# Quartered up products, a ring of chunks and moved side work in a fused retention and mixer kernel

## The chip, the cores and the metric

The kernel runs on one core of a Trainium2 chip. A core has a matrix engine (TensorE, PE in the profile, with its weight loads as PEld), three elementwise engines (VectorE: DVE, ScalarE: ACT, GpSimd: POOL) and SyncE (SP), which here issues DMAs. Each engine runs its own list of instructions in order; semaphores make one wait for another. Matrix products go into PSUM, which has eight banks, each one 128x512 tile of 32-bit floats; the other engines read them from there into SBUF. The metric is the device time of one execution, in microseconds (us), as the median of several runs; lower is better.

## The reference, cut to what matters

```python
def _attn_ref(q, k, v):                      # 8 batches, 8 heads, 576 tokens, 64 dims
    scores = scale * np.matmul(q, k.transpose(0, 1, 3, 2))
    gamma = 1.0 - 2.0 ** (-5.0 - np.arange(H))
    Dmat = np.where(rel >= 0, gamma[:, None, None] ** rel[None, :, :], 0.0)
    return np.matmul(scores * Dmat[None, :, :, :], v)

def _moe_ref(x, U, V, w_ch1, w_ch2):         # x: 8 batches, 576 tokens, 512
    xt = x.transpose(0, 2, 1)
    h = xt @ U @ V                           # rank 32, over the tokens
    u = x + h.transpose(0, 2, 1)
    ch = np.maximum(u @ w_ch1, 0.0) @ w_ch2  # 512 -> 2048 -> 512
    return u + ch
```

So: attention with a decay in place of the softmax gives x; a low-rank mixer over the tokens gives u; two dense layers with a relu between them, the larger part of the work, give the output.

## The kernel before, in words

A batch has 576 tokens, four and a half chunks of 128. Two batches make a *pair* of nine chunks. The dense layers run over *tiles* of four chunks (512 tokens), nine tiles in all, so a tile can lie in one pair or across two.

**The order of the work.** Nothing is reordered on TensorE, VectorE or ScalarE: the program writes the order out by hand. Batches 0 and 1 and tile 0 are written as a list of short steps, `EARLY` (lines 33 to 64), done by `early` (line 605). In it `dn` is the mixer's down product (tokens to rank 32) of a head pair, `at` copies it out of PSUM, `ux` and `uv` build the transposed u of a head pair in PSUM (x through the identity, plus V times the down product), `ua` and `ub` copy it to SBUF. `hu` is the up product of one chunk of batch 0 in the plain layout, `ha` adds x to it, which gives u. `y`, `R`, `M` and `O` are work of tile 0: a first product, a relu, a unit of four matmuls, an output add with its store. `misc` is a list of setup work, mostly on VectorE (`between`, line 1311), `hv` issues the loads of batch 1's k and v on SP's queue.

After that, the loop at line 1343 runs over tiles 1 to 8. Tile j is a list of *units* (`mlp_units`): 16 units of the first layer (four 128x512 products each), then units of the second layer, 16 of four matmuls in tile 1, and 14 in the later tiles, where sums of blocks of the weights and of the first layer's result save products (seven products instead of eight). `sums_of_w2` (line 894) makes those of the weights, six VectorE instructions, once, within tile 1. Into the units the attention of batch j + 1 is threaded: `attention_steps` (line 568) gives each step a number, and a step runs before the unit of that number. A *visit* is the work on a head pair: products of the last pair's values, new states and scores, which VectorE masks. The last visit is followed by the mixer: `mix_middle` (down product), `mix_up_full` (the up product of four chunks) and `mix_up` (the chunk that is half a batch), VectorE's adds of x, and `mix_turn_by_dma`, DMA transposes of u into uT on SP's queue. uT is the first layer's moving operand of the next tile, u is added to its output. What is left of batch 1 (plain u of chunks 4 to 8) is in a list `late`, done within tile 1.

**Rank 32 on a 128-row engine.** From batch 2 on, `mix_up_full` uses `at_diag`: the down product of head pair g lies in rows 32g to 32g+31 and columns 128g to 128g+127, and V is repeated in all four row groups, so each product needs 32 rows only, and four row groups can hold four of them. For batches 0 and 1 the down product lies in `at_sb`, over 128 rows padded with zeros, and an up product takes the whole engine.

**Where u lives.** `pair_pool` holds u and uT of a pair, in two sets that alternate. In a tile across two pairs, `first` (line 943) makes two groups of four products for each unit, one for each pair's chunks (128 and 384, 256 and 256, or 384 and 128 columns), and some later additions of u are split in the same way.

**PSUM banks.** In the loop three banks (`ps_mm`, tag "mm") serve the units, three ("one", tag "att") and two ("two", tag "pss") the attention. A bank is given out in turn; the next user waits until the last reader is done.

Of the kernel before, what the change touches and what calls it, by code (L numbers as in the profile page):

```python
# [14 lines left out]
class Pinned:  # L15
# [52 lines left out]
def kernel(  # L68
# [19 lines left out]
    dm = H * D  # L88
# [44 lines left out]
    pair_pool = ctx.enter_context(tc.tile_pool(name="pair_pool", bufs=2))  # L133
# [168 lines left out]

    def scale_head(b, h):

        x = v_sets[b % NSET][:, :, h, :]
        act.activation(out=x, in_=x, func=AF.Copy, scale=vs64[:, h:h + 1])

    to_scale = []
# [27 lines left out]
    def wait_for_turns(b):  # L336

        chs = chunks_of(b)
        pool.tensor_copy(
            out=landed[:, 0:len(chs)], in_=pairs[b // 2]["uT"][:, chs[0]:chs[-1] + 1, 0, 0]  # L340
        )
# [169 lines left out]
    def mix_up(b, m, x_t, st, pair):  # L511
# [3 lines left out]
        ch = m if b % 2 == 0 else NB - 1 + m  # L515
        dve.tensor_tensor(
            out=pair["u"][lo:hi, ch, :], in0=ps[lo:hi, :], in1=x_t[lo:hi, m, :], op=ALU.add
        )

    def mix_up_full(b, x_t, st, pair):  # L520
# [3 lines left out]
        ps += [banks["one"].tile([P, dm], FP32, tag="att", name="ps_h") for _ in range(2)]  # L524
        first = b % 2
# [8 lines left out]
        ch = 0 if b % 2 == 0 else NB  # L534
        for g in range(NHP):
            cols = slice(g * P, (g + 1) * P)
            dve.tensor_tensor(
                out=pair["u"][:, ch:ch + NB - 1, cols],
                in0=ps[g].rearrange("p (c d) -> p c d", c=NB - 1),
                in1=x_t[:, first:first + NB - 1, cols], op=ALU.add,  # L540
            )

    def mix_turn(ch, pair):
        ps = banks["one"].tile([P, NCC, P], BF16, tag="att", name="ps_ut")
        for cc in range(NCC):
            pe.transpose(ps[:, cc, :], pair["u"][:, ch, cc * P:(cc + 1) * P], ident)
        act.copy(out=pair["uT"][:, ch, :, :], in_=ps)

    def mix_turn_by_dma(chs, pair):

        a, b = chs[0], chs[-1] + 1
        sp.dma_start_transpose(
            out=pair["uT"][:, a:b, :, :].rearrange("p c k t -> p (c k) t"),
            in_=pair["u"][:, a:b, :].rearrange("p c d -> p (c d)"),
        )

    pairs = {}
# [847 lines left out]
```

## Time and profile before

| | us |
|---|---|
| median of 3 runs | 316.35 |
| lowest and highest | 316.05, 318.78 |
| the profiled execution | 315.44 |
| its span, first to last instruction | 313.7 |
| VectorE busy | 227.8 |
| mean DMA rate (GB/s) | 129 |

The profiled execution is one more run; between its time and its span lie 1.74 us of start and end. In a row of the timeline the first number is the start in us from the first instruction, the second the length, then engine, operation, output, inputs and shape; x is the count of merged instructions, and in brackets stands how long the engine had been idle and what released it. "L25" is the line of a helper that records every operation, so groups are told apart by the names of their tiles: `ps_y` and `y_t` are the dense layers, `w_sb` the weights, `kv_runs` from tile 1 on the sums of w2, `ps_b` the PSUM banks of the early list, `xh`, `pss`, `sc` and `ret` the visits, `ps_at` and `ps_h` the mixer, `u_t` and `uT_t` u and its transpose. Matmuls are pipelined: each is shown with a tail that overlaps the next one, and the distance of two starts tells the rate.

### The profile page before, as it was taken

The numbers are of one execution on the slowest core, as the hardware profiler recorded it, in microseconds if no ns is written. First come the engines' busy times: TensorE is split into PE (matmuls) and PEld (weight loads), VectorE is DVE, ScalarE is ACT, GpSimd is POOL, SyncE is SP. The second block draws the span as 40 slices with busy tenths as digits, with TensorE's granted clock in tenths as the row PEclk, the third lists the DMA queues.
The fourth block names the chain that finished last, engine by engine and source line by source line (L and its number), as shares of the span: only waits on it lengthen the run. The fifth ranks groups of instructions, "written<-read, shape, count | busy, mean of one in ns | idle before, by whom it ended". The sixth has DMA issues, their size and how long they took to land.

```text
span 313.7 us, 9760 instructions
## 1 busy us (share of the span) xinstructions
PE 305.0 (97%) x4120; PEld 203.5 (65%) x4120; DVE 227.8 (73%) x551; ACT 163.5 (52%) x338; POOL 136.5 (44%) x177
## 2 busy tenths in 40 slices
PE   8899999999998999999999999999999999999995
PEld 3664456644543677845788888457877884685484
DVE  6877529859997896899689968997799772352244
ACT  7667514367521687267726772678077407504610
POOL 8682339948940971289139812612200220040040
PEclk9999999999999999999999999999999999999999
DMA  8999999999999999599999999994510051012003
GB/s 121 198 206 207 201 204 138 160 178 169 135 149 229 116 148 153 119 170 127 151 203 148 155 135 166 145 149 94 167 36 4 2 154 66 0 34 102 0 2 135
DMA packets 154525, 40.59 MB, mean 129 GB/s; under 512 B 139089, under 2 KB 153457, under 8 KB 154481
## 3 DMA queue, kind: packets, MB, share of 16 engines
q0 software_dynamic: 91344, 17.09, 69.8%
q1 hardware_dynamic: 63136, 22.88, 37.9%
q8 instruction: 32, 0.52, 0.7%
q14 instruction: 13, 0.10, 0.1%
HBM read 36.85 MB, written 9.44 MB: 148 GB/s over the span
## 4 chain that ended last, share of the span: by engine, by line
PE 80%; DVE 7%; DMA 3%; SPq 3%; issue 1%; ACT 0%; DVEq 0%; ACTq 0%
PE ps_y L25 66%; PE xh L25 5%; PE ps_b L25 4%; SPq L25 3%; DVE u_t L25 2%; DMA kv_runs<-in_v_dram 2%; PE sc L25 2%; DMA uT_t<-u_t 2%; PE pss L25 1%; DVE kv_runs L25 1%; PE ps_h L25 1%; DVE v_all L25 1%; DVE o_sb L25 1%; PE ps_at L25 1%; DVE V_sb L25 1%
## 5 line engine op out<-in xcount | busy, mean ns | idle before, releaser
L25 PE MATMUL ps_y<-uT_t,w_sb 128*128 128x512 bf16 (+3 forms) x768 | 130.8, 326 | 1.4 <-DMA uT_t<-u_t 1.4
L25 ACT ACTIVATE y_t<-ps_y 128x512 bf16<-128x512 f32 x144 | 85.6, 597 | 63.5 <-PE ps_y L25 62.4
L25 PEld LDWEIGHTS <-w_sb 128*128 128x128 bf16 x768 | 68.3, 98 | 52.3 <-DMA uT_t<-u_t 1.6
L25 POOL TENSOR_TENSOR o_sb<-o_sb,u_t 128x512 f32<-128x512 f32 (+1 forms) x24 | 24.4, 1034 | 109.4 <-DVE o_sb L25 102.2
L25 PEld LDWEIGHTS <-y_t 128*128 128x128 bf16 x576 | 55.3, 98 | 18.7
L25 PE MATMUL ps_y<-w_sb,y_t 128*128 128x256 bf16 (+1 forms) x352 | 57.7, 311 | 0.0
L25 DVE SCALAR_TENSOR_TENSOR S<-S,keep,pss 128x64 bf16<-128x64 bf16 x168 | 47.0, 280 | 5.1
L25 DVE TENSOR_TENSOR o_sb<-ps_y,o_sb 128x512 f32<-128x512 f32 (+1 forms) x37 | 24.4, 662 | 26.8 <-PE ps_y L25 12.8
L25 DVE TENSOR_TENSOR ret<-sc,qsrow 128x640 bf16<-128x640 f32 x48 | 39.3, 820 | 3.9 <-ACT y_t L25 2.1
L25 PEld LDWEIGHTS <-y_sums 128*128 128x128 bf16 x336 | 32.0, 98 | 4.7
L25 POOL DMA_DIRECT2D k_all<-in_k_dram x36 | 30.8, 859 | 8.9 <-DMA w_sb<-in_moe_w_ch_dram 7.6
L25 POOL DMA_DIRECT2D q_all<-in_q_dram x37 | 28.9, 806 | 4.2 <-DMA w_sb<-in_moe_w_ch_dram 4.2
L25 DVE TENSOR_TENSOR y_sums<-y_t 128x512 bf16<-128x512 bf16 x28 | 11.7, 420 | 22.2 <-ACT y_t L25 22.1
L25 POOL DMA_DIRECT2D v_all<-in_v_dram x31 | 27.3, 888 | 0.5 <-PE ps_y L25 0.2
L25 PE MATMUL ps_y<-w_sb,y_sums 128*128 128x256 bf16 x224 | 27.4, 273 | 0.0
L25 PE MATMUL ps_y<-kv_runs,y_t 128*128 128x256 bf16 x224 | 26.9, 273 | 0.0
L25 ACT ACTIVATE x_t<-xh,xs 128x320 bf16<-128x320 f32 x48 | 22.7, 524 | 7.9 <-PE xh L25 6.2
L25 DVE TENSOR_TENSOR u_t<-ps_h,x_t 128x512 bf16<-128x512 f32 (+1 forms) x35 | 22.3, 682 | 3.0 <-PE ps_h L25 2.8
L25 ACT CAST S<-pss 128x64 bf16<-128x64 f32 x24 | 5.0, 208 | 27.3 <-issue 24.1
L25 ACT ACTIVATE v_all<-v_all,vs 128x320 bf16<-128x320 bf16 x32 | 14.9, 548 | 0.1
L25 POOL COPY landed<-uT_t 128x4 bf16<-128x4 bf16 (+1 forms) x4 | 0.8, 191 | 32.2 <-DMA uT_t<-u_t 32.2
L25 PE MATMUL ps_y<-kv_runs,y_sums 128*128 128x256 bf16 x112 | 13.9, 273 | 0.0
(132 smaller groups left out, 307.7 us busy)
## 6 DMA issues: line engine op xcount, KB each, us to landing
out_dram<-o_sb SPq DMA_DIRECT2D x35, 256.0 KB, 3.0
w_sb<-in_moe_w_ch_dram POOLq DMA_DIRECT2D x8, 512.0 KB, 12.2
v_all<-in_v_dram POOLq DMA_DIRECT2D x25, 128.0 KB, 6.9
k_all<-in_k_dram POOLq DMA_DIRECT2D x24, 128.0 KB, 6.0
q_all<-in_q_dram POOLq DMA_DIRECT2D x20, 128.0 KB, 4.8
q_all<-in_q_dram POOLq DMA_DIRECT2D x12, 144.0 KB, 5.8
given<-in_v_dram SPq DMA_DIRECT2D x8, 128.0 KB, 4.4
kv_runs<-in_v_dram SPq DMA_DIRECT2D x3, 256.0 KB, 6.1
```

The source lines that it names most:

```text
L25: return self._tc.keep_in_program_order(call(*args, **kwargs))
```

## The change

Five edits, in the words of the program:

1. **Up products in row quarters for batches 0 and 1.** In `EARLY`, `hu` and `ha` of chunks 0 to 3 go. A new step `hd` (behind `misc`) copies the four diagonal blocks of `at_sb` into `at_diag[0]` on VectorE; `hf`, between M 10 and M 11, makes the 16 products of `mix_up_full`, into four of the early banks; `hg` adds x. For batch 1, `dn` uses 32 columns of U and writes 32 PSUM rows, `at` copies straight into `at_diag[1]`, and `uv` reads 32 rows; `late` holds `mix_up` of chunk 0 and one `mix_up_full` in place of five `mix_up`.
2. **Two outputs stored later.** In tile 1 the output adds (with their stores) of the second and third rows of the tile run before units 27 and 29, not at the end of units 23 and 27.
3. **Sums of w2** in tile 1 at steps 3.2 and 5.8, not 20.8 and 21.8.
4. **u and uT in rings** of 16 chunks. A chunk's place is its number modulo 16, so a tile's four chunks always lie side by side, and `first` makes four products for each unit in every tile. Batch 3's five chunks wrap around the end: its adds and its `wait_for_turns` come in two parts, and its DMA transposes are of 2, 1 and 2 chunks.
5. **Other banks for one visit.** The last visit of batch 2 (in tile 1) takes its two PSUM banks from "one" and not from `ps_mm`; its mixer starts at step 22 and not 22.3, so the down and the up product run one unit earlier.

On SP's queue the order of issues changes in three places: one store of tile 0 now stands behind the first two q and k transposes of tile 1; the store of the second output of tile 1 stands behind batch 2's transposes of u; and batches 3 and 7 group their chunks differently. The diff, cut to its core:

```diff
-    0 3 DVE; ua 0 3 ACT; y 0 3; R 0; y 1 3; y 2 3; hu 4 4; hu 2 0; R 1; ha 4; hu 1
-    2; hu 0 1; hu 3 3; R 2; M 3; ha 1; ha 2; M 4; R 3; z 3; exv; misc; hv; M 5; R 4;
-    M 6; R 5; M 7; R 6; M 8; ha 0; R 7; ha 3; M 9; R 8; M 10; R 9; M 11; R 10; M 12;
+    0 3 DVE; ua 0 3 ACT; y 0 3; R 0; y 1 3; y 2 3; hu 4 4; R 1; ha 4;
+    R 2; M 3; M 4; R 3; z 3; exv; misc; hd; hv; M 5; R 4;
+    M 6; R 5; M 7; R 6; M 8; R 7; M 9; R 8; M 10; R 9; hf 0 1 2 3; hg; M 11; R 10; M 12;
...
-        pool_, tag = (banks["one"], "att") if last and b >= NTURN else (ps_mm, "mm")
+        pool_, tag = (banks["one"], "att") if last else (ps_mm, "mm")
...
+    def add_quarters(b, x_t, ps):
+
+        first = b % 2
         for g in range(NHP):
             cols = slice(g * P, (g + 1) * P)
...
+            at = 0
+            for a, n in in_ring(chunks_of(b)[first:]):
+                dve.tensor_tensor(
+                    out=ring["u"][:, a:a + n, cols],
+                    in0=ps[g].rearrange("p (c d) -> p c d", c=NB - 1)[:, at:at + n, :],
+                    in1=x_t[:, first + at:first + at + n, cols], op=ALU.add,
+                )
+                at += n
...
+    NRING = 16
+    ring = {
+        "u": consts.tile([P, NRING, dm], BF16, name="u_t"),
+        "uT": consts.tile([P, NRING, NCC, P], BF16, name="uT_t"),
+    }
+
+    def chunk(b, m):
+        return (b // 2 * NCH + b % 2 * (NB - 1) + m) % NRING
...
+            if op == "hd":
+                for g in range(NHP):
+                    r, cols = slice(g * R, (g + 1) * R), slice(g * P, (g + 1) * P)
+                    dve.tensor_copy(out=at_diag[0][r, cols], in_=at_sb[0:R, cols])
+                return
+            if op == "hf":
+                shared["hf"] = [bank(a, [P, dm]) for a in (b, *i)]
+                up_by_quarters(0, {"at": at_diag[0]}, shared["hf"])
+                return
+            if op == "hg":
+                add_quarters(0, x_ts[0], shared["hf"])
+                return
...
-            (up, 0, lambda m=m: mix_up(1, m, x_ts[1], st, pair))
-            for m, up in enumerate((14, 20, 22.8, 28.2, 26.2))
-        ] + [(29, 1, lambda: mix_turn(NCH - 1, pair))]
+            (14, 0, lambda: mix_up(1, 0, x_ts[1], st)),
+            (26, 0, lambda: mix_up_full(1, x_ts[1], st)),
+            (26.5, 0, lambda: mlp1["O"](1)),
+            (28.5, 0, lambda: mlp1["O"](2)),
+            (29, 1, lambda: mix_turn(NCH - 1)),
...
-            for p, c, n in segs:
-                for cc in range(NCC):
-                    pe.matmul(
-                        ps[:, at:at + n * P],
-                        w1_sb[:, cc, f * P:(f + 1) * P],
-                        pairs[p]["uT"][:, c:c + n, cc, :],
-                        start=(cc == 0), stop=(cc == NCC - 1),
-                    )
-                at += n * P
+            for cc in range(NCC):
+                pe.matmul(
+                    ps, w1_sb[:, cc, f * P:(f + 1) * P], ring["uT"][:, own:own + 4, cc, :],
+                    start=(cc == 0), stop=(cc == NCC - 1),
+                )
...
-            elif alone and not sums and part == 3:
+            elif alone and part == 3 and not sums and not (j == 1 and i in (1, 2)):
                 add_and_store(i)
...
-                attention_steps(2, (5, 8.5, 12, 15.5, 21), 1.5, 22.3, 8) + late
-                + [(at, 3, lambda i=i: sums_of_w2(i)) for i, at in enumerate((20.8, 21.8))],
+                attention_steps(2, (5, 8.5, 12, 15.5, 21), 1.5, 22, 8) + late
+                + [(at, 3, lambda i=i: sums_of_w2(i)) for i, at in enumerate((3.2, 5.8))],
```

More of the change, by code (lines that the diff above doesn't have):

```diff
@@ L552, in mix_turn_by_dma @@
         sp.dma_start_transpose(
[L553 to L566 removed]
+            out=ring["uT"][:, a:a + n, :, :].rearrange("p c k t -> p (c k) t"),
@@ new lines, in mix_turn_by_dma, with in_ring @@
+            in_=ring["u"][:, a:a + n, :].rearrange("p c d -> p (c d)"),
+        )
+    NRING = 16
[5 more added lines that the diff above has]
+        return (b // 2 * NCH + b % 2 * (NB - 1) + m) % NRING
+    def chunks_of(b):
+        return [chunk(b, m) for m in range(NB - 1 + b % 2)]
+    def in_ring(chs):
+        runs = []
+        for ch in chs:
+            if runs and sum(runs[-1]) == ch:
+                runs[-1][1] += 1
+            else:
+                runs.append([ch, 1])
+        return runs
@@ L847, in step @@
             elif op == "at":
-                copy(out=at_sb[:, cols], in_=st["d"])
+                copy(out=at_diag[1][rank, cols] if b else at_sb[:, cols], in_=st["d"])
             elif op == "ux":
@@ L918, in y1 @@
             return held["y1"]
[L920 to L926 removed]
+        own = 4 * j % NRING
         sums = j >= 2
```

106 lines of the change are left out of this document (37 added, 69 removed).

## The prediction

> **What bounds the kernel now.** I read the page's first block and chain, then TensorE's waits, then the busy time of each engine by stage.
>
> ```profile
> PE 305.0 (97%) x4120; PEld 203.5 (65%) x4120; DVE 227.8 (73%) x551; ACT 163.5 (52%) x338; POOL 136.5 (44%) x177
> PE 80%; DVE 7%; DMA 3%; SPq 3%; issue 1%; ACT 0%; DVEq 0%; ACTq 0%
> PE ps_y L25 <- DMA uT_t<-u_t: 1.4, 1, 1.4
> PE xh L25 <- DVE o_sb L25: 0.3, 1, 0.3
> 43.50:63.10 19.60, 19.06 (x339) 12.75 (x339) 15.66 (x30) 8.02 (x19) 17.09 (x24) 1.00 1.53 160
> 132.76:163.95 31.19, 31.19 (x469) 20.51 (x473) 26.12 (x58) 19.21 (x41) 17.73 (x22) 1.00 1.66 158
> 163.95:195.28 31.33, 31.33 (x533) 26.79 (x537) 26.31 (x58) 19.20 (x41) 18.37 (x22) 1.00 1.52 156
> ```
>
> TensorE is busy 305.0 of 313.7 us at a granted clock of 1.00 (the number before the DMA share in the stage rows); 80% of the chain is its own. From tile 3 on (the last two rows: length of the stage, then TensorE's busy time) it has no gap at all. So time can be won only by taking matmuls away, or from the gaps before tile 2: 1.4 us where tile 2 waits for the transposed u, 0.3 us where the last visit of tile 1 waits for a PSUM bank that an output add holds, and 19.60 - 19.06 = 0.54 us in the stretch of batch 1's attention. The other 7% and 3% of the chain (DVE, DMA) say where a delay on DVE would cost.
>
> **The change part by part.** I follow one number, how late TensorE is against before (minus is early), through four places.
>
> *Batch 0's up product (27 to 43 us).* Four of the five 128x512 products go, 16 of 32x128 come, later, after eight units of M. Ahead of those 16 VectorE must now copy the four diagonal blocks, and these copies stand behind the whole setup list ("misc").
>
> ```profile
> 24.28 1.24 PE L25 MATMUL ps_b<-at_sb,V_sb 128*128 128x512 bf16 x5
> 25.36 10.96 PE L25 MATMUL ps_y<-uT_t,w_sb 128*128 128x512 bf16 x50
> 24.10 1.57 ACT L25 ACTIVATE y_t<-ps_y 128x512 bf16<-128x512 f32 x3 [1.08 <-PE ps_y L25]
> 24.75 1.88 DVE L25 TENSOR_TENSOR u_t<-ps_b,x_t 64x512 bf16<-64x512 f32 x3 [1.58 <-ACT y_t L25]
> 28.09 1.91 DVE L25 COPY V_sb<-V_sb 32x576 bf16<-32x576 bf16 x7
> 33.96 0.09 DVE L25 MEMSET mask<- 64x32 uint32 x1
> 44.10 0.76 DVE L25 TENSOR_TENSOR qz<-ps_b,qsrow 128x576 bf16<-128x576 bf16 x1 [7.47 <-PE ps_b L25]
> 124.24 0.33 PE ps_h L25 x16
> 120.25 1.75 PE ps_y L25 x16
> 122.39 1.85 PE ps_y L25 x16
> ```
>
> Five products take 25.36 - 24.28 = 1.08 us, 0.216 each, so M 3 could start 0.86 us earlier; but it takes the bank of the first of the three relus that start at 24.10, done near 24.62, and starts some 0.1 behind that, at 24.72: 0.64 early. 50 matmuls in 10.96 us less a tail of 0.17 are 0.863 us per unit of four; eight units end at 24.72 + 6.91 = 31.63. VectorE ended the setup list at 34.05. Two adds fewer (1.88/3 = 0.63 each) make that 32.8; four copies of 32x128 cost at most 0.27 each (the 32x576 copies, 1.91/7), by their columns 0.06; nearer to the small instructions around them I take 0.10: 33.2. So TensorE waits some 1.57 us where it did not wait before; between 0 (if the list runs faster) and 2.2. Then the 16 small products: 0.33 us, the price of the same 16 in tile 2, and 0.10 on the matmuls behind them (16 matmuls take 1.85 us after such a group, 1.75 otherwise). M 11 starts at 33.2 + 0.43 = 33.63 against 25.36 + 6.91 = 32.27: 1.37 late. Nothing queued behind it on TensorE can pass; ScalarE's relus and the output adds of tile 0 follow it. VectorE's four 128x512 adds replace two and lie in its idle stretch of 7.47 us before 44.10, for nothing; they would cost 4 x 0.63 = 2.5 us if that cover were gone.
>
> *Batch 1's attention (43 to 63 us).* The 0.54 us of gaps here end with VectorE's work on v, which follows loads that SP issues after that setup list; the list now ends 0.85 earlier there, so the gaps swallow lateness: 1.37 - 0.54 = 0.83. The down products with 32 columns and up products with 32 rows keep their count: two adjacent up products in different row groups may overlap (-0.2), six or so more changes of tiling cost up to +0.6; I take 0, as this stretch is full of 64-wide shapes anyway.
>
> *Tile 1 (63 to 102 us).* The sums of w2 go from VectorE's late stretch to its head.
>
> ```profile
> 63.28 0.69 DVE L25 TENSOR_TENSOR o_sb<-ps_y,u_t 128x512 f32<-128x512 f32 x1 [0.92 <-PE ps_y L25]
> 63.89 1.50 DVE L25 TENSOR_SCALAR qsrow<-mask 128x128 f32<-128x128 bf16 x8
> 66.66 1.56 DVE L25 TENSOR_TENSOR v_all<-v_all,vs 128x640 bf16<-128x640 bf16 x2 [1.28 <-DMA v_all<-in_v_dram]
> 70.32 0.82 DVE L25 TENSOR_TENSOR ret<-sc,qsrow 128x640 bf16<-128x640 f32 x1 [2.09 <-ACT y_t L25]
> 86.13 0.82 DVE L25 TENSOR_TENSOR ret<-sc,qsrow 128x640 bf16<-128x640 f32 x1
> 87.60 0.32 PE L25 MATMUL xh<-S,qz 64*64 64x64 bf16 x15 [0.30 <-DVE o_sb L25]
> 88.78 0.69 DVE L25 TENSOR_TENSOR kv_runs<-kv_runs,w_sb 128x1024 bf16<-128x1024 bf16 x1
> 92.41 0.40 PE L25 MATMUL ps_h<-at_diag,V_sb 32*128 32x128 bf16 x16
> 93.36 3.07 DVE L25 TENSOR_TENSOR u_t<-ps_h,x_t 128x512 bf16<-128x512 f32 x5
> 93.19 1.00 SPq L25 DMA_DIRECT2D out_dram<-o_sb  x2
> 95.87 4.07 SPq L25 DMA_TRANSPOSE uT_t<-u_t  x2
> 97.15 4.80 DMA uT_t<-u_t
> 101.99 2.25 PE L25 MATMUL ps_y<-uT_t,w_sb 128*128 128x384 bf16 x18 [1.42 <-DMA uT_t<-u_t]
> ```
>
> Six sums at 0.69 are 4.1 us; the idle time there is 1.28 + 2.09 = 3.4. In order: the last add of tile 0 at 63.28 + 0.83 = 64.1, mask tables to 65.6, three sums to 67.65, two scalings to 69.15, three sums to 71.2, then the first mask, at 70.32 before: 0.9 late, and 0.07 more than TensorE itself. From this mask to the one at 86.13 VectorE has hardly a gap and every visit waits for it, so TensorE is 0.9 late at the last visit, whatever it was before. (This also means that most of an early gain would be lost here.)
>
> Then the bank: the visit now takes other banks, -0.30. The two output adds stored later hold their banks until units 27 and 29, while unit 28 takes the first output's bank, free long before: 0; it would cost a wait of one 0.69 us add. Batch 1's four 128x512 products (0.86) become one group of 16 (0.33 + 0.10): -0.43. Two new waits are tight, the down product on the last x (one unit less lies between them) and the transpose of chunk 8 on batch 1's adds, each 0 to 0.3: +0.2 in all. TensorE would reach tile 2 0.37 late, 100.9 instead of 100.57 (101.99 - 1.42).
>
> The transposed u of batch 2: its up product comes one unit earlier, 92.41 - 0.86 + 0.5 = 92.05; no sum of w2 and no add of batch 1 is ahead on VectorE; four adds (3.07/5 = 0.61) end near 94.5 instead of 95.8. The second transpose starts 1.28 behind the first (95.87, 97.15), at 95.8, and took 4.8 us: 100.6. The queue of SP is a gain here too (one store less ahead) and a loss (a store of tile 0 stands now among the q and k transposes; 0.5 each, by 93.19). So the wait of 1.42 goes, TensorE itself is next late; of the landing time I take all 4.8. At tile 2: 0.37 - 1.42 = -1.05.
>
> *Rings (tiles 2, 4, 6).* 64 units lose four of eight matmuls each in three tiles, 192 less. Tile 4 (two halves) took 31.33 against 31.19 of the whole tile 3: 0.14. Tile 2 is:
>
> ```profile
> 99.76:132.76 33.00, 31.58 (x534) 24.15 (x537) 27.57 (x61) 19.21 (x41) 16.89 (x22) 1.00 1.32 146
> 226.44:257.60 31.16, 31.16 (x526) 24.43 (x526) 26.22 (x58) 15.28 (x33) 3.71 (x5) 1.00 0.16 42
> ```
>
> 33.00 - 1.42 = 31.58, 0.39 over tile 3; tile 6 shows 31.16, nothing. Sum 0.53, with bounds 0.15 and 0.55; I take -0.5. Batch 3's adds become eight smaller ones and VectorE has time there. All in all -1.05 - 0.5 = -1.55 us: 315.44 (313.7 of span and 1.74 around it) becomes 313.9 in the profiled execution, and the median 316.35, 0.91 above it, becomes 314.8.
>
> **A row and a rule.** By the groups of the page a split unit looks dearer:
>
> ```profile
> L25 PE MATMUL ps_y<-uT_t,w_sb 128*128 128x512 bf16 x384 | 86.7, 379 | 0.0
> L25 PE MATMUL ps_y<-uT_t,w_sb 128*128 128x128 bf16 x128 | 12.4, 219 | 0.0
> ```
>
> 12.4/128 = 97 ns against a quarter of 86.7/384, 56 ns. The busy time of a short matmul holds its modelled tail, and the stage rows above contradict it, so I keep 0.5. The Trainium skill (TensorE: Matmul & The Clock Gate, Back-to-back issue gap) gives about 81 ns for a 128-column matmul in a stream with weight loads; by that, as an estimate, tiles 2 and 6 would gain 128 x 25 ns = 3.2 us instead of 0.4. Tile 6's 31.16 us shows none of it.
>
> **The rivals.** *All gains stay* (0.25): VectorE is ready at the small products, so the 1.57 us wait is gone and TensorE stays 0.2 early; the sums of w2 fill only idle time, and the masks start earlier with TensorE. Then 0.64 - 0.43 + 0.54 (gaps) + 0.30 + 0.43 + 1.42 + 0.5 = 3.4 without the small new waits: 313.0. For it: the idle time at the head of tile 1 is almost the sums' length. Against: the setup list ends at 32.8 by the rows, and the 1.28 us there end with a load that no edit hastens.
>
> *The wait only moves* (0.15): the transposes of batch 2, in a queue of DMAs that is full in this stretch, land no earlier than 101.95 whatever their start. Then tile 2 starts as before and only the rings gain: 316.35 - 0.5 = 315.9. For it: 4.8 us of landing here. Against: nothing else of SP's is in front of them now but one store.
>
> *Slower* (0.2): the sums at the head of tile 1 are not covered. v's load lands at 66.66; if it or the sums are late, the masks start later by all of the six sums, 4.1 us, and each visit of tile 1 with them: 314.8 + 4.0 = 318.8. It decides from 1.55 us of uncovered work on. GpSimd issues loads at the new place:
>
> ```profile
> 64.16 0.88 POOL L25 DMA_DIRECT2D v_all<-in_v_dram  x1 [0.24 <-PE ps_y L25]
> 88.58 0.88 POOL L25 DMA_DIRECT2D v_all<-in_v_dram  x1
> 91.56 0.69 DVE L25 TENSOR_TENSOR kv_runs<-w_sb,kv_runs 128x1024 bf16<-128x1024 bf16 x1
> ```
>
> If the two hinder each other there and a sum takes 0.82 instead of 0.69, 6 x 0.13 more bring it to 319.6. Against: the sum at 88.78 beside such an issue and the one at 91.56 without any took the same 0.69. The rule that speaks against the change is the Trainium skill's (GPSIMD Engine Reference, Specifications): GpSimd shares SBUF interfaces with those VectorE instructions that have two SBUF inputs, as the sums do. These two rows don't bear it out.
>
> **How the numbers follow.** The forecast (0.4) is 314.8 (313.3 to 316.2 with the bounds above); "all gains" lies at 313.0, "only moves" at 315.9, "slower" at 318.8. The range 312.6 to 317.4 leaves out most of "slower" (0.15) and little below. One per cent, about what a measurement of this kernel can tell from no change, is 3.16 us: faster by more is "all gains", 0.25; slower by more is half of "slower", 0.1; the rest 0.65.
>
> **What would show it.** A wait of TensorE on VectorE near 31.6 of some 1.5 us (none: "all gains"); the first mask of tile 1 near 71.2 rather than 70.3 (74 or later: "slower"); no wait on the transposed u at tile 2's start, which comes near 101 (still 1.4: "only moves"); tile 2 and tile 4 within 0.1 us of tile 3. The forecast is wrong in its main term if the wait at the small products isn't there or if VectorE's saturation in tile 1 doesn't hold TensorE.

## The result and the profile after

The changed kernel takes 318.49 us (median of 20 runs, 316.68 to 322.6) where the kernel before takes 316.81 in the same comparison (20 runs): ratio 1.0055, 95% interval 1.0033 to 1.0077. It is slower by half a per cent, 1.7 us; forecast were 1.55 us less, and 318.49 lies above the range of 312.6 to 317.4. The profiled execution took 318.43 us with a span of 316.7; it is 2.99 above the one before because that one lay 1.37 under its kernel's median of 316.81, while this one lies at its own.

The page's first block and the clock row of its 40 slices:

```profile
PE 307.1 (97%) x3937; PEld 190.2 (60%) x3952; DVE 229.4 (72%) x558; ACT 163.5 (52%) x338; POOL 137.8 (43%) x175
...
PEclk9999799999999999999999999999999999999999
```

TensorE has 183 matmuls fewer in the records (3937 against 4120) and is busy 2.1 us longer. One slice of the clock row shows 7. Both say that some matmuls ran slower. TensorE's timeline around the sixteen small products (start, length, operation, shape, count, idle time before and its releaser):

```profile
24.48 0.38 PE L25 MATMUL ps_b<-at_sb,V_sb 128*128 128x512 bf16 x1
...
33.30 1.02 PE L25 MATMUL ps_b<-at_diag,V_sb 32*128 32x128 bf16 x16 [1.30 <-DVE at_diag L25]
34.26 6.18 PE L25 MATMUL ps_y<-uT_t,w_sb 128*128 128x512 bf16 x20
40.28 5.99 PE L25 MATMUL ps_y<-w_sb,y_t 128*128 128x512 bf16 x26
```

The wait on the copies is there, 1.30 us. The sixteen products are spread over 0.96 us (33.30 to 34.26) because VectorE hands the four blocks over one at a time. Then comes the surprise: the twenty matmuls of five units take 40.28 - 34.26 = 6.02 us, and five units took 5 x 0.863 = 4.31 before. The busy times by stretch show why; the number before the last two of each row is the granted clock:

```profile
34.30:35.50 1.20, 1.20 (x5) 0.43 (x5) 0.93 (x5) 0.00 (x0) 0.51 (x1) 0.68 1.24 207
35.50:36.50 1.00, 1.00 (x4) 0.43 (x3) 1.00 (x2) 0.60 (x1) 0.26 (x1) 0.50 1.28 203
36.50:37.50 1.00, 1.00 (x4) 0.33 (x3) 1.00 (x3) 0.03 (x1) 0.00 (x0) 0.50 1.30 198
37.50:38.50 1.00, 1.00 (x4) 0.39 (x3) 0.32 (x2) 0.57 (x1) 0.91 (x2) 0.68 1.28 195
```

The clock stood at half. If the two stretches of 0.68 are a mixture of 1.00 and 0.50, the half clock lasted 0.77 + 1 + 1 + 0.64 = 3.41 us and cost half of that, 1.71 us: just the 6.02 - 4.31.

VectorE and GpSimd at the head of tile 1 (the third fence is GpSimd in the kernel before):

```profile
67.11 0.69 DVE L25 TENSOR_TENSOR o_sb<-ps_y,u_t 128x512 f32<-128x512 f32 x1 [0.82 <-PE ps_y L25]
...
68.80 0.68 DVE L25 TENSOR_TENSOR kv_runs<-w_sb 128x1024 bf16<-128x1024 bf16 x1
69.51 1.42 DVE L25 TENSOR_TENSOR kv_runs<-kv_runs,w_sb 128x1024 bf16<-128x1024 bf16 x1
...
71.58 2.40 DVE L25 TENSOR_TENSOR v_all<-v_all,vs 128x640 bf16<-128x640 bf16 x2
...
75.95 0.82 DVE L25 TENSOR_TENSOR ret<-sc,qsrow 128x640 bf16<-128x640 f32 x1
```

```profile
68.70 1.69 POOL L25 TENSOR_TENSOR v_all<-v_all,vs 64x512 bf16<-64x512 bf16 x1 [3.77 <-ACT y_t L25]
...
72.21 1.08 POOL L25 TENSOR_TENSOR v_all<-v_all,vs 128x512 bf16<-128x512 bf16 x1
```

```profile
68.74 1.04 POOL L25 TENSOR_TENSOR v_all<-v_all,vs 64x512 bf16<-64x512 bf16 x1 [3.71 <-ACT qz L25]
...
72.98 1.04 POOL L25 TENSOR_TENSOR v_all<-v_all,vs 128x512 bf16<-128x512 bf16 x1 [1.43 <-DMA v_all<-in_v_dram]
```

One sum takes 1.42 us where the others take 0.69, and the two scalings of v take 2.40 where they took 1.56; each lies on a scaling that GpSimd does at that moment (68.70 to 70.39, 72.21 to 73.29), and the first of GpSimd's takes 1.69 instead of 1.04 as well. Not every meeting lengthens VectorE's part: the sum at 68.80 lies within GpSimd's first scaling and keeps its 0.68. So from the last output add of tile 0 to the first mask there are 75.95 - 67.11 = 8.84 us, where the forecast had 71.2 - 64.1 = 7.1. TensorE's rows of tile 1, and the length and busy times of tiles 2 and 4:

```profile
66.91 4.48 PE L25 MATMUL ps_y<-uT_t,w_sb 128*128 128x512 bf16 x20
...
77.11 2.01 PE L25 MATMUL xh<-S,qz 64*64 64x64 bf16 x16
78.91 0.33 PE L25 MATMUL pss<-v_all,k_all 64*64 64x64 bf16 x16
...
92.50 0.32 PE L25 MATMUL xh<-S,qz 64*64 64x64 bf16 x16
```

```profile
104.72:136.00 31.28, 31.23 (x461) 20.56 (x462) 27.33 (x64) 19.24 (x41) 16.72 (x21) 1.00 1.32 131
...
167.19:198.36 31.17, 31.12 (x461) 20.52 (x461) 26.23 (x58) 19.18 (x41) 18.52 (x23) 1.00 1.69 164
```

At 77.11 the second visit stops within its group: 1.80 us to the next, where an unhindered one takes 0.15 (92.50 has no stop, and no wait for a bank either). Tiles 2 and 4 took 33.00 and 31.33 us before; now they take 31.28 and 31.17, without a wait for the transposed u.

How late TensorE is against before, at the places that the prediction followed:

| place | before, after (us) | late | step measured | step forecast |
|---|---|---|---|---|
| the up product of chunk 4 | 24.28, 24.48 | 0.20 | 0.20, a later start, no edit | 0 |
| M 11 | 32.27, 34.26 | 1.99 | +1.79 | +1.37 |
| five units on | 36.58, 40.28 | 3.70 | +1.71 | 0 |
| first down product of batch 1 | 54.74, 57.84 | 3.10 | -0.60 | -0.54 |
| first uT products in tile 1 | 63.08, 66.91 | 3.83 | +0.73 | 0 |
| last visit of tile 1 | 87.60, 92.50 | 4.90 | +1.07 | +0.07 - 0.30 |
| tile 2 | 99.76, 104.72 | 4.96 | +0.06 | -0.43 + 0.2 |
| tile 3 | 132.76, 136.00 | 3.24 | -1.72: wait 1.42, ring 0.30 | -1.42 - 0.4 |
| end of the span | 313.7, 316.7 | 3.0 | -0.2: tile 4 0.16 | -0.14 |

### The profile page after: what moved, and what is told of

It reads as the page before. It is cut to its first block, busy times and chain, and to the rows that moved or that the text cites. A ratio compares the mean times of both kernels' runs of the same rounds, so it can differ in the third digit from the quotient of the medians.

```text
span 316.7 us, 9418 instructions
## 1 busy us (share of the span) xinstructions
PE 307.1 (97%) x3937; PEld 190.2 (60%) x3952; DVE 229.4 (72%) x558; ACT 163.5 (52%) x338; POOL 137.8 (43%) x175
## 4 chain that ended last, share of the span: by engine, by line
PE 85%; DVE 5%; DMA 3%; POOL 1%; issue 1%; DVEq 0%
PE ps_y L25 70%; PE xh L25 5%; PE ps_b L25 5%; DMA v_all<-in_v_dram 3%; PE sc L25 2%; PE pss L25 1%; POOL v_all L25 1%; PE ps_h L25 1%; DVE v_all L25 1%; PE ps_at L25 1%; DVE V_sb L25 1%; DVE S L25 1%; POOL k_all L25 1%; DVE ret L25 0%; DVE kv_runs L25 0%
## 5 line engine op out<-in xcount | busy, mean ns | idle before, releaser
L25 PE MATMUL ps_y<-uT_t,w_sb 128*128 128x512 bf16 x576 | 132.0, 383 | 0.2
L25 PEld LDWEIGHTS <-w_sb 128*128 128x128 bf16 x576 | 54.8, 99 | 62.8 <-issue 2.6
L25 POOL TENSOR_TENSOR o_sb<-o_sb,u_t 128x512 f32<-128x512 f32 x21 | 24.0, 1152 | 109.7 <-DVE o_sb L25 104.1
L25 PE MATMUL ps_y<-w_sb,y_t 128*128 128x256 bf16 (+1 forms) x344 | 56.1, 310 | 0.7 <-issue 0.5
L25 DVE TENSOR_TENSOR u_t<-ps_h,x_t 128x512 bf16<-128x512 f32 (+2 forms) x39 | 22.3, 627 | 5.4 <-PE ps_h L25 5.1
L25 POOL COPY landed<-uT_t 128x4 bf16<-128x4 bf16 (+3 forms) x5 | 0.9, 188 | 34.4 <-DMA uT_t<-u_t 34.4
```

Source lines behind the costliest of these rows:

```text
L25: return self._tc.keep_in_program_order(call(*args, **kwargs))
```

## The experiments

Each was timed in five rounds beside the kernel before on the same chip. The ratios are to the kernel before, with 95% intervals; the four comparisons ran on four chips, so rows of different ones are better compared by ratio than by median.

| run | median us (12 runs) | ratio | profiled span | clock of it |
|---|---|---|---|---|
| rings alone | 316.88 | 1.0024 (0.9989 to 1.0058) | 315.2 | 0.997 |
| changed, sums back | 316.65 | 1.0017 (0.9991 to 1.0043) | 315.5 | 1.00 |
| changed, products later | 317.04 | 1.0012 (0.9979 to 1.0045) | 315.4 | 1.00 |
| changed, both | 316.37 | 0.9994 (0.9963 to 1.0025) | 314.0 | 1.00 |
| both, `uv` over 128 rows | 316.06 | 0.9989 (0.9965 to 1.0014) | 316.0 | 0.988 |
| changed, wide products | 318.38 | 1.0068 (1.0034 to 1.0102) | 315.4 | 1.00 |
| products later, sums split in tile 1 | 316.70 | 1.0000 (0.9963 to 1.0036) | 315.2 | 1.00 |
| products later, sums split over two tiles | 317.23 | 1.0030 (0.9995 to 1.0066) | 314.8 | 1.00 |
| before, fewer loads in tile 1 | 315.28 | 0.9972 (0.9941 to 1.0003) | 314.3 | 1.00 |
| changed, fewer loads | 318.00 | 1.0028 (0.9985 to 1.0071) | 320.5 | 0.984 |
| both, `uv` over 128 rows, fewer loads | 315.33 | 0.9978 (0.9942 to 1.0015) | 313.2 | 0.998 |
| split over two tiles, 128 rows, fewer loads | 317.55 | 1.0031 (0.9998 to 1.0065) | 316.3 | 0.995 |
| before, rings and fewer loads | 315.31 | 0.9956 (0.9927 to 0.9986) | 314.5 | 0.996 |
| the same, sums early | 317.00 | 1.0026 (0.9994 to 1.0058) | 315.0 | 1.00 |

The kernel before had 316.29, 316.32, 316.30 and 316.19 in the four comparisons (the first four rows, the next four, the next four, the last two). Intervals of 0.3% are a microsecond, so a single pair of medians under 1 us apart shows little; where a smaller step is told below it comes from the profile.

**Undoing the two costs, one at a time and together.** The sums go back to their place; the small products go behind four more units.

```diff
-                + [(at, 3, lambda i=i: sums_of_w2(i)) for i, at in enumerate((3.2, 5.8))],
+                + [(at, 3, lambda i=i: sums_of_w2(i)) for i, at in enumerate((20.8, 21.8))],
```

> The changed kernel with the sums of w2 back at steps 20.8 and 21.8 of tile 1. Theory (the sums at the head of tile 1 meet GpSimd's scaling of v, and hold the masks): the stop of some 1.75 us at the second visit goes, sums and scalings take 0.69 and 0.78 again, and the sums now fill VectorE's gap of 3.57 us before batch 2's adds, which end at most 0.6 us later; 1.2 to 1.7 us faster than the changed kernel, 317 in the median. Rival (TensorE's slack swallows it, or the wait for the transposed u comes back at tile 2): within 0.4 us of the changed kernel.

```diff
-    R 9; hf 0 1 2 3; hg; M 11; R 10; M 12; R 11; M 13; R 12; M 14; R 13; M 15;
+    R 9; M 11; R 10; M 12; R 11; M 13; R 12; M 14; R 13; hf 0 1 2 3; hg; M 15;
```

> The changed kernel with batch 0's 16 small products and their adds four units later (behind M 14 and not M 10). Theory (the wait for VectorE's copies costs 1.3 us, 0.6 more within the group, and the gap brings the clock down for some 3.4 us): no wait of TensorE there, granted clock 1.00 in this stretch, and 1.5 to 3.3 us gained there; of it some is lost again at the second visit of tile 1, where VectorE's sums decide, so 1 to 2.5 us faster than the changed kernel. Rival (the clock drops for another reason, the small products themselves): the clock still shows 0.5 to 0.7 behind them and only 1.3 to 1.9 us are gained there.

> Both edits of the two runs before together. Theory: the two costs stand one behind the other on TensorE, so they add: 3 to 4.5 us faster than the changed kernel, 314 to 315.5, faster than the kernel before by 0.5 to 1 per cent. Rival (one wait hides the other): no better than the better of the two alone, within 0.4 us.

By the ratios (1.0055 for the changed kernel) each alone takes 1.2 and 1.4 us off, as each theory said; together they take off 1.9, not the 3 or more of the theory. The ratio of the two together is 0.9994, so they account for the loss; what the other edits gain doesn't show. The timelines say why. With the sums back (first fence) the stop of the second visit is gone, and with the products later (second fence, the run with both) the group has no wait; but with the sums back the wait at tile 2 is there again:

```profile
33.30 0.64 PE L25 MATMUL ps_b<-at_diag,V_sb 32*128 32x128 bf16 x3 [1.28 <-DVE at_diag L25]
...
75.91 0.32 PE L25 MATMUL xh<-S,qz 64*64 64x64 bf16 x16
...
PE ps_y L25 <- DMA uT_t<-u_t: 1.4, 1, 1.4
```

```profile
35.74 0.40 PE L25 MATMUL ps_b<-at_diag,V_sb 32*128 32x128 bf16 x16
...
102.52 3.61 PE L25 MATMUL ps_y<-uT_t,w_sb 128*128 128x512 bf16 x16 [1.14 <-DVE ret L25]
...
PEld L25 <- DMA uT_t<-u_t: 1.2, 1, 1.2
```

In the second the releaser is named as VectorE's mask, which ended at 102.43; but these products don't need it: in the run with both, 128 rows and fewer loads they start at 101.57, before that mask (101.88). The weight load's row beneath it names the transfer. The run with the products later alone has this wait too, 1.67 us. The changed kernel had lost it only because TensorE came to tile 2 five microseconds late. The clock stayed at 1.00 in the first of these profiles, behind the same 1.28 us wait, so the drop doesn't come every time.

**Rings alone**, on the kernel before.

```diff
-            "u": pair_pool.tile([P, NCH, dm], BF16, tag="u_t", name="u_t"),
-            "uT": pair_pool.tile([P, NCH, NCC, P], BF16, tag="uT_t", name="uT_t"),
+        "u": consts.tile([P, NRING, dm], BF16, name="u_t"),
+        "uT": consts.tile([P, NRING, NCC, P], BF16, name="uT_t"),
```

> The kernel before with the rings alone (192 matmuls fewer; the early list, the sums, the late products and the banks as before). Theory (the ring gains, the waits lose): tiles 2, 4 and 6 become as long as tile 3, some 0.4 to 0.5 us in all, the wait of 1.4 us at tile 2 stays; ratio to before 0.998 to 0.999. Rival (the rings themselves, or the store that moved on SP's queue, cost the time): as slow as the changed kernel, ratio near 1.005.

Not resolved: 1.0024 with an interval on both sides of 1. The gain of tiles 2 and 4 is in the table above (0.30 + 0.16 us), but it lies behind the wait for uT, which didn't stay at 1.4 as expected: it is 2.66 us in this profile.

**Wide products at the same place**: the changed kernel with batch 0's group as four products over 128 rows.

```diff
-                up_by_quarters(0, {"at": at_diag[0]}, shared["hf"])
+                for m, ps in enumerate(shared["hf"]):
+                    pe.matmul(ps, V_sb[0][:, m * P:(m + 1) * P], at_diag[0], start=True, stop=True)
```

> The changed kernel, with batch 0's up product at the same place as four products of 128x512 over all 128 rows and four whole-row adds, so the wait for the four at_diag copies stays and the sixteen small products are gone. Theory: the granted clock of 0.50 that the changed kernel's profile shows behind that wait comes from the 1.3 us gap, in some executions only; then some runs here too have a mean granted clock under 0.995, the products take 4 x 0.22 = 0.87 us instead of 0.33, and the median is 0.2 to 0.6 us over the changed kernel's 318.0 or so. Rival: the mix of narrow and wide products drops the clock; then the mean clock is 1.00 in all runs and the median is not over the changed kernel's. Both expect a wait of about 1.3 us for at_diag.

```profile
34.07 1.04 PE L25 MATMUL ps_b<-at_diag,V_sb 128*128 128x512 bf16 x3 [2.04 <-DVE at_diag L25]
```

With no small products the median is the changed kernel's (318.38), so it isn't their narrowness that costs. The wait is 2.04 us, not the 1.3 that both sides expected: each wide product reads all four blocks and so waits for the last copy, and M 11 starts at 34.94, 0.68 later than in the changed kernel's profile. On the clock the run decides less: it stayed at 1.00 behind this longer wait; 4 of its 12 executions had a mean clock of at most 0.996, against 12 of 20 of the changed kernel.

**Tiling.** In the run with both edits, batch 1's stretch is still longer than before. `uv` is taken over all 128 rows, as it was:

```diff
-                        at_diag[1][rank, cols] if b else at_sb[:, cols],
-                        V_sb[b][rank if b else slice(0, P), a * k * P:(a + 1) * k * P], start=False, stop=True,
+                        at_diag[1][:, cols] if b else at_sb[:, cols],
+                        V_sb[b][:, a * k * P:(a + 1) * k * P], start=False, stop=True,
```

> The sums of w2 back at 20.8 and 21.8, batch 0's products behind M 14, and batch 1's uv products taken over all 128 rows, so that TensorE does not change its row tiling between its small groups. Theory: the 0.7 us that batch 1's stretch gained in length is the draining of TensorE at each change of tiling; ratio to the kernel before 0.9970 to 0.9985 (315.4 to 315.9), 0.5 to 0.7 us under the run with these two edits alone. Rival: the loss comes from the width of the products (dn now has 32 columns) or from the copies; then no difference from that run, 316.2 to 316.6.

316.06 against 316.37 is not resolved. The starts of the second down group and of the last three `uv` in the timelines of the kernel before, of the run with both, and of the run with 128 rows and fewer loads:

```profile
57.58 0.44 PE L25 MATMUL ps_b<-x_t,U_sb 128*128 128x128 bf16 x5
60.92 0.60 PE L25 MATMUL ps_b<-V_sb,at_sb 128*128 128x512 bf16 x3
```

```profile
58.43 0.45 PE L25 MATMUL ps_b<-x_t,U_sb 128*32 128x128 bf16 x5
62.39 0.39 PE L25 MATMUL ps_b<-V_sb,at_diag 32*128 32x512 bf16 x3
```

```profile
58.25 0.45 PE L25 MATMUL ps_b<-x_t,U_sb 128*32 128x128 bf16 x5
62.02 0.60 PE L25 MATMUL ps_b<-V_sb,at_diag 128*128 128x512 bf16 x3
```

3.34, 3.96 and 3.77 us for the same sequence. About a third of the loss goes with the 32 rows of `uv` (0.19 of 0.62), less than the 0.5 to 0.7 expected. The same timelines put the rest at the 32 columns of `dn`: in the run with 128 rows, the two `dn` that stand between 128-wide products start 0.09 and 0.10 us later behind their neighbours than before, and each takes 0.39 us to the next start where it took 0.28. So a change to or from a 32-wide shape costs about 0.1 us here. The Trainium skill (TensorEngine Tiling (Array Packing), Key Properties) says that a change of the tiling mode drains TensorE; these rows agree with it, some 0.1 us a change.

**Where the wait for uT comes from.** First the sums were split, so that none stands ahead of batch 2's adds on VectorE: three at the head of tile 1, three behind the adds or in tile 2.

```diff
-                + [(at, 3, lambda i=i: sums_of_w2(i)) for i, at in enumerate((20.8, 21.8))],
+                + [(at, 3, lambda i=i: sums_of_w2(i)) for i, at in enumerate((3.2, 30.5))],
```

> The sums of w2 split: the first three at 3.2 in tile 1, where VectorE stands idle for 2.5 us ahead of the first mask, the other three at 30.5, behind batch 2's adds; batch 0's products behind M 14. Theory: in the run with all six at 20.8 and 21.8 the adds of batch 2 stand 1.1 to 1.4 us behind the sums, and with them the transposes of u, so the wait for uT at tile 2 comes back; with the split it is gone, the ratio is 0.9960 to 0.9980 (315.0 to 315.7), and tile 2's first y products follow without a gap. Rival: the three late sums hold VectorE in front of the output adds and the first masks of tile 2, and a wait for a PSUM bank of about 1 us takes the place of the wait for uT: 316.2 to 316.8.

```diff
+                + [(3.2, 3, lambda: sums_of_w2(0))],
...
+            steps += [(1.5, 3, lambda: sums_of_w2(1))]
```

> As the run before, with the second three sums at 1.5 in tile 2, ahead of the last sum of w2. Theory: 315.0 to 315.7, no wait for uT, and tile 2's visits keep up because VectorE had 0.3 us of idle time and more there. Rival: 2.07 us more on VectorE between the first masks of tile 2 and its S terms stop TensorE for about 1.8 us at a visit: 316.5 to 317.

In the first the wait for uT is gone, as the theory had it, and the rival's number came true beside it: 316.70. The late sums make a visit of tile 2 stop (the row at 106.24, 0.63 to the next work of the visit instead of 0.15), and the tile takes 32.2 us between its first uT product (102.68) and the next tile's (134.89), where 31.2 is the rule. Besides, a scaling of v on VectorE took 2.41 us beside one of GpSimd, and a visit of tile 1 stopped (the row at 79.94, 0.97 to the next work):

```profile
75.62 2.41 DVE L25 TENSOR_TENSOR v_all<-v_all,vs 128x640 bf16<-128x640 bf16 x1
```

```profile
76.27 1.06 POOL L25 TENSOR_TENSOR v_all<-v_all,vs 128x512 bf16<-128x512 bf16 x1
```

```profile
79.94 1.18 PE L25 MATMUL xh<-S,qz 64*64 64x64 bf16 x16
...
106.24 0.84 PE L25 MATMUL xh<-S,qT_all 64*64 64x64 bf16 x16
```

In the second neither theory came true. Batch 2's adds ran as early as they can (they waited for TensorE, first row below), and yet the wait for uT grew to 2.10 us. So VectorE was not its cause. The transposes' own rows (lengths at SP's queue, and issue to landing) in that run:

```profile
92.74 4.88 DVE L25 TENSOR_TENSOR u_t<-ps_h,x_t 128x512 bf16<-128x512 f32 x8 [3.58 <-PE ps_h L25]
103.28 3.61 PE L25 MATMUL ps_y<-uT_t,w_sb 128*128 128x512 bf16 x16 [2.10 <-DMA uT_t<-u_t]
L25 SPq DMA_TRANSPOSE uT_t<-u_t x2: 1819/2612/3405, 95.8 to 99.3; - x2
DMA to landing us min/median/max: 3.9/5.2/6.5
```

In the changed kernel they landed after 2.9 and 4.0 us, in the kernel before after 4.8 and 5.2. The same two transposes take between 2.7 and 6.5 us. What is different is what else the transfer engines carry. In the run with 128 rows, whose loads are as before, TensorE was late and the transposes were issued at 98.5 us, with the transfer engines idle since 96.4: they landed in 2.8 us. To test it directly, the loads were made fewer: of the three blocks of batch 4's k and v that tile 1 brings in, two go to tile 2.

```diff
-            load_batch(4, range(3))
+            load_batch(4, range(1))
+            while to_scale:
+                scale_block(NRUNS, to_scale.pop(0))
...
-            ahead = {4: 3, 5: 3, 6: 3, 7: 4}
+            ahead = {4: 1, 5: 3, 6: 3, 7: 4}
```

> The kernel before, with two of the three blocks of batch 4's k and v that tile 1 loads (4 x 128 KB) moved to tile 2. Theory: uT lands when the transfer engines, full until 98 us, come free; half a megabyte less in front of it lets it land about 2 us sooner, the wait of 1.4 us at tile 2 is gone, and the ratio is 0.994 to 0.997 (314.5 to 315.5). Rival: uT lands a fixed time after batch 2's adds, whatever is loaded; then the wait stays, and the ratio is 0.999 to 1.002; a third: the loads moved to tile 2 are late for tile 3, a wait there of 1 us or more, 317 and up.

The busy share of the transfer engines from 88 to 104 us, in 40 slices of 0.4 us and in tenths, before and with fewer loads:

```profile
DMA  9999999999999999999999899990029999995000
uT_t<-u_t SPq DMA_TRANSPOSE x2, 5.0
```

```profile
DMA  9999999999980690978700000994699791019529
uT_t<-u_t SPq DMA_TRANSPOSE x2, 2.8
```

Before, they are full until 98.8 us, and the transposes, issued at 95.9 and 97.2, share them; with half a megabyte less they are no longer full from 92.4 us on, and the transposes land in 2.8 us. The wait for uT at the start of tile 2 is gone (first uT products at 101.09 without idle time ahead, 101.99 before), and the median is 1.0 us under the kernel before, the interval just reaching 1.0003. A part of the wait has only moved on: the loads now run in tile 2, batch 3's transposes land after 4.1 us there, and tile 3's first uT products wait 1.15 us in this profile (its row again names VectorE's mask; the second of the transposes, issued at 129.5 and landing 4.0 to 4.1 us later, is done just then, near 133.6). That is the third case of the expectation in part, with the transposes late there and not the loads.

> The changed kernel with the same two blocks moved. Its profile has no wait for uT, because TensorE is 3 us late there; so by the theory nothing is gained: 1.0035 to 1.0070, 317.4 to 318.6, as the changed kernel. Rival: the loads slow something else in tile 1 (a visit, VectorE), and the time falls by 1 us or more.

318.00: as the theory said, the changed kernel gains nothing that can be told, since it has no wait there. Its profiled execution took 322.19 us at a mean clock of 0.984, so its timeline is not compared.

> Sums of w2 back at 20.8 and 21.8, batch 0's products behind M 14, batch 1's uv products over 128 rows, and the two blocks moved. Theory: without the wait for uT the savings of the rings and of the smaller products show: 0.993 to 0.997, 314.2 to 315.4. Rival: the time stays with the kernel without the move, 0.9965 to 1.0015, because the adds behind the sums set when uT lands.

315.33, level with the kernel before with fewer loads (315.28). The transposes land in 2.8 us here too, so the sums ahead of the adds do no harm once the engines are free, against the rival, though the ratio lies in its range. The three removals won nothing that shows over the loads' edit alone.

> As the run before, with the sums split: three at 3.2 in tile 1, three at 1.5 in tile 2. Theory: its uT wait of 2.1 us in the run with the loads in place came from the full transfer engines; with the move it is under 0.5 us, and the time 313.8 to 315.2 (0.992 to 0.996). Rival: the three sums at the head of tile 1 meet GpSimd's scaling of v and block a visit, 0.8 to 1.6 us, 315.5 to 316.5.

The transposes land in 2.8 us, tile 2 starts earliest of all, at 100.97, and the time is 317.55, above both forecasts. The loss is in tile 2: the three sums hold VectorE at the second visit, and there the clock falls again.

```profile
108.92 2.34 PE L25 MATMUL xh<-S,qT_all 64*64 64x64 bf16 x16
...
111.94 5.30 PE L25 MATMUL ps_y<-uT_t,w_sb 128*128 128x512 bf16 x16
```

```profile
111.00:112.00 1.00, 0.95 (x49) 0.81 (x49) 1.00 (x2) 0.37 (x2) 1.00 (x3) 0.99 2.34 149
112.00:113.00 1.00, 1.00 (x7) 0.35 (x4) 0.97 (x3) 0.79 (x2) 1.00 (x3) 0.50 2.41 153
...
115.00:116.00 1.00, 1.00 (x5) 0.38 (x4) 0.96 (x4) 0.45 (x1) 1.00 (x2) 0.80 1.75 163
```

Sixteen matmuls take 117.18 - 111.94 = 5.24 us instead of 3.5. The half clock (0.50 in each of the three stretches from 112 to 115) lasts 0.02 + 3.00 + 0.40 = 3.42 us, as at 34.7 us in the changed kernel.

**The early sums by themselves**, on the kernel before with rings and fewer loads.

> The kernel before with the rings alone, and the two blocks of batch 4's k and v moved to tile 2, so that no transfer holds uT back. Theory: the rings give back the 0.4 us by which tiles 2 and 4 ran over 31.17 us: 0.3 to 0.5 us under the run of the kernel before with the blocks moved, 314.5 to 315.2 (0.994 to 0.997), each of tiles 2 to 5 at 31.2 us from its first uT product to the next tile's. Rival: the rings change nothing that can be seen, 315.0 to 315.8.

```diff
-                + [(at, 3, lambda i=i: sums_of_w2(i)) for i, at in enumerate((20.8, 21.8))],
+                + [(at, 3, lambda i=i: sums_of_w2(i)) for i, at in enumerate((3.2, 5.8))],
```

> As the run before it, with the sums of w2 at 3.2 and 5.8 of tile 1 as in the changed kernel, and nothing else of it: the price of the early sums by itself. Theory: they hold VectorE at the first masks, the second visit of tile 1 stops TensorE for 1.1 to 1.7 us, and nothing later gives that back: 1.1 to 1.7 us over the run with rings and moved blocks alone, and 1.7 us more in executions where the granted clock falls behind the stop. Rival: the stop was the fault of TensorE's other delays in the changed kernel; then this run is not over that one by more than 0.5 us.

315.31 and 317.00: the early sums cost 1.7 us by themselves, with the clock at 1.00 in the profile, as the theory said. The first row is from the run without them, the others from the run with them:

```profile
71.17 0.82 DVE L25 TENSOR_TENSOR ret<-sc,qsrow 128x640 bf16<-128x640 f32 x1 [2.80 <-ACT S L25]
```

```profile
71.37 1.48 DVE L25 TENSOR_TENSOR kv_runs<-kv_runs,w_sb 128x1024 bf16<-128x1024 bf16 x1
...
73.49 0.82 DVE L25 TENSOR_TENSOR ret<-sc,qsrow 128x640 bf16<-128x640 f32 x1
```

```profile
75.73 0.94 PE L25 MATMUL xh<-S,qz 64*64 64x64 bf16 x16
```

Again one sum meets a scaling on GpSimd (0.69 becomes 1.48), the first mask comes 2.3 us later (0.96 of that is a later end of tile 0 in this execution), and a visit stops: 0.73 us to its next row (76.46). Stops of 0.46 and 0.63 us stand at the same place in the two other profiles with all six sums early (products later, wide products), so the 1.80 of the changed kernel's is the longest and no typical one. What the rings are worth isn't resolved (medians 315.31 with and 315.28 without them, ratios 0.9956 and 0.9972); the kernel before with rings and fewer loads is the only run whose interval lies below 1.

## Why the prediction was wrong

**The sums at the head of tile 1** were the step that failed most: forecast at 0.07 us beyond TensorE's own lateness, they cost 1.7 by the last two runs. The prediction put the first mask "0.9 late, and 0.07 more than TensorE itself", and took TensorE to be "0.9 late at the last visit, whatever it was before". The mask came 5.63 late and the last visit 4.90. The first error is the price: 7.1 us from tile 0's last add to the mask were 8.84, and 1.57 of the difference are the sum at 1.42 and the scalings at 2.40 that met GpSimd. The prediction had weighed this contention and dropped it on two sums, one beside a *DMA issue* of GpSimd and one beside nothing; those rows say nothing on an arithmetic instruction of GpSimd, and the scalings of v at 68.74 and 72.98 of the old trace, the ones the sums were moved onto, were not looked at. The Trainium skill's rule (GPSIMD Engine Reference, Specifications) was right: the sums have two SBUF inputs, and so do the scalings. The early sums aren't the only way to such a meeting: in the run with both and 128 rows, with the sums back but TensorE late, the two scalings took 2.39 as well. The second error is "whatever it was before": VectorE's run of masks has hardly a gap, but its work here begins with tile 0's last output add, which TensorE releases (67.11 against 63.28, 3.83 late), so what was lost earlier is passed on and not absorbed. The rival "slower" had the right place and its sign came true (the first mask at 74 or later), though it wanted it from a late load and at the whole length of the sums; that its 318.8 is near the 318.49 measured is luck, since much of the lateness came from the other steps.

**Batch 0's products.** The wait was forecast at 1.57 and is 1.30, but each copy takes 0.20 us, not the 0.10 that the prediction took between 0.06 and 0.27, so the group is fed slowly and takes 0.96 instead of 0.43. M 11 was 1.79 late beyond the later start, not 1.37: the mechanism right, the size within the bounds given. Moved behind four more units, the products wait for nothing, and the ratio falls from 1.0055 to 1.0012.

**The clock** was not in the sum. The prediction read a clock of 1.00 everywhere and took a wait at its length. Here the wait was followed by 3.41 us at half clock, 1.71 us more. That belongs to the account of this profile and is not needed for the medians: the eight executions of the changed kernel with a mean clock of 0.997 or more have a median of 317.8 us, the 91 such ones of the kernel before in the four comparisons (on other runs and chips) 316.1, so without drops the difference is 1.7 as well.

**Batch 1's shapes** were put at 0 between -0.2 and +0.6; they cost 0.73, beyond the upper bound, by the changes of shape shown above. The gaps absorbed 0.60, forecast 0.54. Batch 1's up product in tile 1, put at -0.43 with +0.2 for two new waits, came out at +0.06: its sixteen products take 0.52 us to the next start (98.47 to 98.99) and not 0.43, and batch 2's down product 0.69 (94.01 to 94.70) where it took 0.39.

**The transposed u.** The wait went, as forecast, for the wrong reason. The prediction "of the landing time" took "all 4.8" as a constant and let uT land earlier with an earlier start. With TensorE earlier the wait was back, at 1.4 us with the sums back, 1.7 with the products later, 1.1 with both, 2.1 with the sums split over two tiles and 2.7 with the rings alone: the landing is set by the transfer engines, full until 98.8 us, and the rival "the wait only moves" named the cause. The runs with fewer loads show it.

**Rings and bank.** Tiles 2 and 4 gained 0.30 and 0.16 us (forecast 0.39 and 0.14), and the last visit's bank wait of 0.30 is gone. These steps were right in the profile ("64 units" should be 48, sixteen in each of three tiles; the 192 matmuls are right).

The forecast's sum was -1.55. With the measured steps it is +0.20 + 1.79 + 1.71 - 0.60 + 0.73 + 1.07 + 0.06 - 1.42 - 0.46 = 3.1, against 3.0 measured in the span of the profiled executions.

## What to carry to other kernels

Before work is moved into an engine's idle time, list what the engine next to it executes there: VectorE's operations on two SBUF tensors became up to twice as long and more beside GpSimd's arithmetic, and idle time for 3.4 us did not hold 4.1 us of sums. A wait for a transfer is not bought off by starting the transfer earlier while the transfer engines are full; look at their busy share in that stretch first, and move a load that nobody needs yet. A wait that disappears from a profile may be gone only because the engine that waited now comes later, so test a saving on a version in which nothing else is late.

## What the hardware showed

- **Half a clock after a short gap.** A wait of 1.30 us followed by a sparse group (0.96 us), and a visit stopped for 2.0 us, were followed by 3.41 and 3.42 us at a granted clock of 0.50, 1.7 us lost each time. The Trainium skill (TensorE: Matmul & The Clock Gate, Part 1) has the clock fall after an idle window of some 3.4 us; the length of the drop agrees with such a window, but here a window with work in it was enough. The same kind of wait passed without a drop in other profiles (1.28, 2.04 and 2.10 us), so it may depend on how the gap lies in the window; this was not settled. Nor does a drop need a gap that an edit made: in the profile of the run with both and 128 rows (clock 0.988) the half clock lies between 14 and 22 us (granted clock 0.94 from 14 to 15, 0.50 to 21, 0.64 to 22), 0.12 + 6.00 + 0.72 = 6.84 us or twice 3.42, around and behind waits of 1.03 and 1.30 us for the first loads and GpSimd's work on v, which come ahead of every edit. A mean clock of at most 0.996, which one such drop gives (1.71 of 316 us is 0.5%), was found in 12 of 20 executions of the changed kernel, in 37 of 128 of the kernel before, and in 5 of 60 of the five kernels with both edits or with fewer loads whose profiles show no wait over 1.2 us after the early list's first loads. That fits drops that come with waits, but doesn't show it.
- **GpSimd and VectorE on SBUF.** Where their arithmetic met, VectorE's 0.69 us became 1.42 and 1.48, its 1.56 for two became 2.40, GpSimd's 1.04 became 1.69; VectorE's masks and state updates, which read PSUM, kept 0.82 and 0.31 a piece beside it. Most lengths fit one waiting for the other's end: the sum at 68.80 kept 0.68 while GpSimd's instruction of 68.70 took 0.65 longer, and the second scaling of 71.58 ends 0.69 behind GpSimd's (73.98, 73.29). One doesn't fit: a scaling went from 0.82 to 2.41 beside a GpSimd instruction of 1.06. No run tested it by itself.
- **Transposes by DMA.** The same two took 2.7 to 2.8 us to land with free transfer engines and 3.6 to 6.5 with full ones.
- **Changes of shape on TensorE.** Five 128x128 products with 32 columns of weights, between 128-wide ones, took 0.39 us to the next start where the same with 128 columns took 0.28, and a change to or from a 32-wide shape added about 0.1 us.
